# Windowed attention, forward and backward on one core: DMA-turned P and dS at both ends, reordered first loads and tail, W copies shared with VectorE

## The chip, the core and the metric

The kernel runs on one core of a Trainium2 chip. A core has a matrix engine (TensorE, PE in the profile, with its weight loads shown apart as PEld), a vector engine (VectorE, DVE), a scalar engine (ScalarE, ACT), GpSimd (POOL) and a sync engine (SyncE, SP) that only issues transfers. ACT and POOL also issue transfers, each from its own queue. Matrix products land in PSUM, from where DVE or ACT copies them to SBUF, the on-chip memory.

The metric is the time of one execution on the device in microseconds (us). The profile is one execution recorded by the hardware profiler.

## The reference

Input `x` is an image of 256 x 256 positions with 384 channels, in bf16. It is cut into 1024 windows of 8 x 8 positions, 64 tokens each, and every window attends to itself with one head of 384 channels. The outputs are the forward result and the gradients of x, wqkv and wo for a given `grad_out`:

```python
xw = windows(x)                       # (1024, 64, 384)
qkv = xw @ wqkv
q, k, v = qkv[..., :C], qkv[..., C:2 * C], qkv[..., 2 * C:]
p = softmax(einsum('bqc,bkc->bqk', q, k) * C ** -0.5)
out = unwindow(einsum('bqk,bkc->bqc', p, v) @ wo)
...
_out, _vjp = jax.vjp(_f, x, wqkv, wo)
_grads = _vjp(grad_out)
```

## The kernel before

**The algebra.** The four weight blocks are folded first. `A` is the scaled product of the q and k blocks and `B` that of the v block with wo; their transposes are `AT` and `BT`. With them scores are x A x^T, and the kernel never forms q, k and v. In the code, `z` and `y` are projections of grad_out and x (lines 155-167), `uq` and `vq` are x times B and x times AT (`uv`, lines 227-235), `sd` holds scores and dP together (`scores`, lines 180-187), `P` is the softmax, D its row sum with dP, and dS the gradient of the scores (`soft`, lines 192-225).

**The tiling.** Four pairs of windows make a quad: a tile of 128 partitions (two windows of 64 tokens) times QUAD = 4. There are 128 quads. In most tiles of a quad the lower 64 partitions (LO) belong to the first window of a pair and the upper 64 (HI) to the second.

**The pipeline.** Step i works on three quads at once: attention of quad c = i - 1, scores, softmax and uv of quad b = i, and projections of quad a = i + 1 (`step`, lines 346-387). The order in which each engine does things is written out by hand: the whole body stands under a manual schedule, and each engine runs its instructions in the order in which the program issues them. A step starts with `scores` of b on PE; then follow the eight uv products with softmax between them on DVE and ACT; the three z products of a; the last softmax stage and `turn` (lines 237-245); the loads of quad i + 3; the three y products; one row of weight-gradient products when there is one (`gf_rows`, 308-314, `pg` in the profile); and attention of c, four rounds t = 0 to 3 (`attend`, 254-298). `attend` computes three banks a round, `pw`, `pu` and `po`, and an edge bank `pd`. pw is copied to Wq by ACT (line 280), pu to Uq by DVE (line 283), po to the output by ACT (273), and pd by DVE and ACT in turn.

**PSUM.** All products take their banks from one ring of eight (line 58). When a bank isn't yet copied out, the next product that needs it waits.

**Turning tiles.** Attention needs P and dS of a quad in transposed form, `PS`. Before, DVE makes it from `ps` (P and dS side by side) in five transposes of 32 x 32 blocks (lines 240 and 244). The transposed x and grad_out (`xT`, `dT`) come from DMA transposes on SP (`load_turn`, 135-141); for the first quads from PE transposes instead, with copies by `copy_out` that alternate between DVE and ACT (`turn_on_pe`, 143-148). G_ON_PE = 4 says that dT of quads 0 to 3 is made on PE, X_ON_PE = 1 that xT of quad 0 is. Token-major z and y (`tok`) come from one larger DMA transpose on SP a quad (`to_tokens`, 175-178), of 24 blocks of 128 x 128; xT and dT have 12 blocks.

**SP's queue in step i** is: dT and xT of quad i + 2, tok of quad i, and two of the four x loads of quad i + 3. The other two x loads are on ACT after y's copies (`load_rest`). POOL issues the grad_out loads (dq) and the stores. Each of these waits in order on its queue.

**Weight gradients.** Three finished quads form a group (GQ = 3). Each group leaves six rows of products, put into `fill` (line 472) when its last quad's attention is done. Each later step takes one by `gf_rows` and one spread over the attention rounds in half tiles (`gf_halves`, `ph` in the profile); DVE adds them to GF_acc in f32. The first group is complete at the end of step 3, so steps 0 to 3 have no such products. What is left after the last step is done in the `while fill` loop, and the last two quads' share in `gf_final`; `weight_gradients` (399-434) then forms the two weight gradients and stores them.

**The start** (lines 437-452): the weight loads, nine products on zeros that keep PE busy (`warm_up`), the loads of quads 0 to 2, the BT product, the PE turns of quad 0, the A product, the clearing of GF_acc. The loop starts at i = -1, which does only the projections of quad 0. B and AT are computed by `weight_rest` in step 0, between scores and uv (line 355).

Of the kernel before, what the change touches and what calls it, by code (L numbers as in the profile page):

```python
# [14 lines left out]
P = 128  # L15
# [8 lines left out]
def kernel(  # L24
# [50 lines left out]
    def fetch_weights():  # L75
        nc.sync.dma_start(out=w_sb[:, :, columns(2)], in_=w_in[:, :, columns(2)])
        nc.scalar.dma_start(out=wo_sb[:], in_=wo.rearrange("(m p) n -> p m n", p=P))
        for k in (0, 1):
            nc.scalar.dma_start(out=w_sb[:, :, columns(k)], in_=w_in[:, :, columns(k)])

# [31 lines left out]
    def weight_rest():  # L112
        weight_product(B_sb, wT[2], wo_sb, None)
        weight_product(AT_sb, wT[1], wT[0], scale)

# [5 lines left out]
    OTHER = {0: HI, WT: LO}  # L121

    def load(st, on_act=0):
        st["xq"] = xq = grp.tile([P, QUAD, C], BF16, tag="xq", name="xq", bufs=2 * GQ + 4)
        st["dq"] = dq = qp.tile([P, QUAD, C], BF16, tag="dq", name="dq", bufs=6)
        for t in range(QUAD):
            if t < QUAD - on_act:
                nc.sync.dma_start(out=xq[:, t, :], in_=windows(x, st, 2 * t))
            nc.gpsimd.dma_start(out=dq[:, t, :], in_=windows(grad_out, st, 2 * t))  # L129

    def load_rest(st, on_act):
# [60 lines left out]
    def soft(st, step):  # L192
# [23 lines left out]
        elif step == 4:  # L216
            st["pr"] = pr = sm.tile([P, QUAD, WT], F32, tag="pr", name="pr")
            for w, h in ((0, LO), (1, HI)):
                nc.vector.tensor_tensor(out=pr[h, :, :], in0=sd[h, :, w, :], in1=st["Pb"][h, :, :], op=ALU.mult)  # L219
            st["D"] = D = sm.tile([P, QUAD], F32, tag="D", name="D")  # L220
            nc.vector.tensor_reduce(out=D[:], in_=pr[:], axis=AX.X, op=ALU.add)
        else:
            pd = sm.tile([P, QUAD, WT], F32, tag="pd")
            nc.vector.tensor_tensor(out=pd[:], in0=st["Pb"], in1=over_k(st["D"][:]), op=ALU.mult)
            nc.vector.tensor_tensor(out=st["dS"], in0=st["pr"][:], in1=pd[:], op=ALU.subtract)

# [10 lines left out]
    def turn(st):  # L237
        ps = st["ps"]
        st["PS"] = dst = qp.tile([P, 2, QUAD, WT], BF16, tag="PS", name="PS")
        nc.vector.transpose(out=dst[:].rearrange("p s t k -> p (s t k)"), in_=ps[:].rearrange("p s t k -> p (s t k)"))  # L240
        for first in range(0, P, WT):
            for q in (0, SQ):
                k = SQ - q
                nc.vector.transpose(out=dst[first + k:first + k + SQ, :, :, q:q + SQ].rearrange("p s t k -> p (s t) k"),  # L244
                                    in_=ps[first + q:first + q + SQ, :, :, k:k + SQ].rearrange("p s t k -> p (s t) k"))

    def operand(st, n, t, h):
        if n in ("PT", "ST"):
            return st["PS"][h, int(n == "ST"), t, :]
        if n in ("z", "y"):  # L250
# [3 lines left out]
    def attend(st, t):  # L254
# [24 lines left out]
        slot(pw, ("Pb", "dq"), ("Pb", "z"), start=True)  # L279
        copies[EV["W"][t]](out=st["Wq"][:, t, :], in_=pw[:])  # L280
        pu = bank("pu")
# [64 lines left out]
    def step(c, b, a, ahead):  # L346


        def on(st):
            return (lambda f, *r: f(st, *r)) if st is not None else (lambda f, *r: None)  # L350
        C_, B, A = on(c), on(b), on(a)
        B(scores)
        B(soft, 0)
        if b is not None and c is None:
            weight_rest()
        B(uv, 0, 0)
# [20 lines left out]
        if ahead is not None:  # L377
            load_rest(ahead, ON_ACT)
        if fill:
            gf_rows(*fill.pop(0))  # L380
        slots = attention(c) if c is not None else iter(())
# [6 lines left out]

    G_ON_PE, X_ON_PE = 4, 1
    ON_ACT = 2  # L390
    EV = {"z": "AAA", "y": "AAA", "u": "AAAA", "v": "AAAA", "o": "AAAA", "U": "DDDD", "W": "AAAA", "d": "DADAA"}
    quads = [(row, col) for col in range(0, W, WIN) for row in range(0, H, 2 * WIN * QUAD)]
    sts = [{"at": q, "i": i} for i, q in enumerate(quads)]
    n = len(sts)
    AHEAD = 3
# [3 lines left out]
    def weight_gradients(group):  # L399
# [32 lines left out]
        for k in range(CK):  # L432
            product_row(k, dw[:, k, :], GFT[1], woT_sb, None)
            (nc.scalar, nc.sync)[k % 2].dma_start(out=dw_out[:, k, columns(2)], in_=dw[:, k, :])

    with tc.manual_schedule(engines=MANUAL):
        fetch_weights()
        warm_up(9)
        load(sts[0])
        make_identity(nc, ident[:])  # L440
        load(sts[1])
        load(sts[2])
# [4 lines left out]
        turn_on_pe(sts[0], "dq", "dT")  # L447
        turn_on_pe(sts[0], "xq", "xT")
        turn_blocks(wT[0], w_sb, 0)
        turn_blocks(wT[1], w_sb, CK)  # L450
        weight_product(A_sb, wT[0], wT[1], scale)
        nc.vector.memset(GF_acc[:], 0.0)
        held = []
        last = None
        get = lambda i: sts[i] if 0 <= i < n else None
        for i in range(-1, n + 1):
            if 0 <= i < n - 2:
                load_turn(sts[i + 2])
            if 0 <= i < n:
                to_tokens(sts[i])  # L460
            step(get(i - 1), get(i), get(i + 1), get(i + AHEAD) if i >= 0 else None)
            if 0 < i + 2 < G_ON_PE:
                turn_on_pe(sts[i + 2], "dq", "dT")
            if i == 1:
# [42 lines left out]
```

## Time and profile before

| | us |
|---|---|
| runs shown | 1910.97, 1917.22, 1922.25 (median 1917.22) |
| profiled execution, whole time | 1913.78 |
| its span, first to last instruction | 1912.0 |
| first scores (quad 0) start | 18.30 |
| scores of quads 1, 2, 3, 4 start | 30.5, 46.55, 59.87, 74.69 |
| scores of quads 5 and 6 start | 89.25, 103.82 |
| scores of quad 127 start | 1868.49 |
| first product of step 128 | 1883.5 |
| last attention product | 1889.6 |

| DMA transposes by SP | median us from issue to landing |
|---|---|
| tok | 10.3 (6.2 to 15.6) |
| xT | 7.6 (4.1 to 11.4) |
| dT | 7.2 (4.5 to 10.9) |

How to read it: an engine's busy time is the time in which it executes; a mean near the span doesn't say what a single step waits for. Rows of the timeline give start and length in us, the engine, the line of the kernel, the operation with output<-input, and its shapes; in brackets stands how long the engine was idle before it and what released it. "PEclk" is the granted clock of the matrix engine as a share of full speed. SPq and ACTq are transfers being issued; the time in such a row is the issue, not the transfer. The span is shorter than the whole time of its execution by 1.8 us.

### The profile page before, as it was taken

The numbers are of one execution on the slowest core, as the hardware profiler recorded it, in microseconds if no ns is written. First come the engines' busy times: TensorE is split into PE (matmuls) and PEld (weight loads), VectorE is DVE, ScalarE is ACT, GpSimd is POOL, SyncE is SP. The second block draws the span as 40 slices with busy tenths as digits, with TensorE's granted clock in tenths as the row PEclk, the third lists the DMA queues.
The fourth block names the chain that finished last, engine by engine and source line by source line (L and its number), as shares of the span: only waits on it lengthen the run. The fifth ranks groups of instructions, "written<-read, shape, count | busy, mean of one in ns | idle before, by whom it ended". The sixth has DMA issues, their size and how long they took to land.

```text
span 1912.0 us, 57287 instructions
## 1 busy us (share of the span) xinstructions
PE 1897.3 (99%) x22359; PEld 1131.5 (59%) x22359; DVE 1676.1 (88%) x3625; ACT 1530.4 (80%) x3357; POOL 860.0 (45%) x1574
## 2 busy tenths in 40 slices
PE   8999999999999999999999999999999999999998
PEld 5556655655665565556556655655665565556555
DVE  6888888888888888888888888888888888888887
ACT  7878887888788888878887887888788788878884
POOL 3444544444444444444444444444444444445432
PEclk9999999999999999999999999999999999999999
DMA  8999999999999999999999999999999999999993
GB/s 183 200 223 215 221 211 214 232 210 222 200 232 211 225 204 229 217 223 216 224 210 212 225 226 219 206 220 221 223 214 216 223 224 204 210 231 222 206 197 93
DMA packets 943376, 406.91 MB, mean 213 GB/s; under 512 B 825344, under 2 KB 918528, under 8 KB 943104
## 3 DMA queue, kind: packets, MB, share of 16 engines
q1 hardware_dynamic: 830352, 226.46, 77.1%
q0 software_dynamic: 75264, 151.11, 32.6%
q10 hardware_dynamic: 37488, 25.67, 6.0%
q8 instruction: 175, 2.87, 0.7%
q14 instruction: 97, 0.79, 0.1%
HBM read 101.84 MB, written 101.84 MB: 107 GB/s over the span
## 4 chain that ended last, share of the span: by engine, by line
PE 95%; DVE 2%; DMA 1%; ACT 1%; issue 0%; ACTq 0%; SPq 0%
PE pj L151 50%; PE pg L151 13%; PE ph L324 13%; PE sd L151 5%; PE pw L269 5%; PE po L269 4%; PE pu L269 4%; DMA dT<-dq 1%; PE pd L269 1%; DMA xq<-in_x_dram 0%; DVE PS L244 0%; ACTq L133 0%; PE pe L403 0%; DVE pr L219 0%; DVE Uq L283 0%
## 5 line engine op out<-in xcount | busy, mean ns | idle before, releaser
L289 POOL DMA_DIRECT2D out_dram<-o x512 | 274.4, 536 | 795.4 <-ACT o L273 783.6
L280 ACT CAST Wq<-pw 128x384 bf16<-128x384 f32 x512 | 246.6, 482 | 280.7 <-PE pw L269 264.9
L151 PEld LDWEIGHTS <-xT 128*128 128x128 bf16 x3072 | 292.3, 98 | 182.9 <-issue 1.0
L129 POOL DMA_DIRECT2D dq<-in_grad_out_dram x512 | 270.6, 534 | 194.5 <-PE pj L151 86.8
L151 PE MATMUL pj<-B_sb,xT 128*128 128x384 bf16 x1536 | 334.0, 327 | 0.0
L151 PE MATMUL pj<-AT_sb,xT 128*128 128x384 bf16 x1536 | 333.8, 326 | 0.0
L283 DVE CAST Uq<-pu 128x384 bf16<-128x384 f32 x512 | 283.1, 553 | 16.9 <-PE pu L269 4.9
L291 POOL DMA_DIRECT2D out_dram<-d x480 | 277.8, 579 | 16.3 <-ACT uq L235 6.6
L151 PE MATMUL pj<-dT,BT_sb 128*128 128x512 bf16 x1152 | 269.5, 379 | 0.0
L151 PE MATMUL pj<-xT,A_sb 128*128 128x512 bf16 x1152 | 269.5, 379 | 0.0
L269 PE MATMUL pd<-tok,ps 64*64 64x384 bf16 x2048 | 256.4, 327 | 0.7 <-ACT Wq L280 0.6
L165 ACT CAST yz<-pj 128x512 bf16<-128x512 f32 x384 | 224.8, 586 | 37.2 <-PE pj L151 28.6
L273 ACT CAST o<-po 128x384 bf16<-128x384 f32 x512 | 249.3, 487 | 3.8 <-PE po L269 3.6
L235 ACT CAST vq<-pj 128x384 bf16<-128x384 f32 x512 | 247.1, 483 | 3.7 <-PE pj L151 0.5
L235 ACT CAST uq<-pj 128x384 bf16<-128x384 f32 x512 | 244.4, 477 | 3.6 <-PE pj L151 1.8
L167 ACT CAST yz<-pj 128x512 bf16<-128x512 f32 x384 | 225.1, 586 | 23.5
L244 DVE STREAM_TRANSPOSE PS<-ps 32x256 bf16<-32x256 bf16 x512 | 223.2, 436 | 9.7
L151 PEld LDWEIGHTS <-xq 128*128 128x128 bf16 x1572 | 153.6, 98 | 115.0 <-issue 0.6
L324 PEld LDWEIGHTS <-xq 64*64 64x64 bf16 x6000 | 177.5, 107 | 67.0
L324 PE MATMUL ph<-Wq,xq 64*64 64x384 bf16 x3984 | 204.4, 322 | 0.0
L151 PEld LDWEIGHTS <-A_sb 128*128 128x128 bf16 x1152 | 112.7, 98 | 135.9
L151 PEld LDWEIGHTS <-BT_sb 128*128 128x128 bf16 x1152 | 112.7, 98 | 122.3
(85 smaller groups left out, 3066.1 us busy)
## 6 DMA issues: line engine op xcount, KB each, us to landing
dq<-in_grad_out_dram POOLq DMA_DIRECT2D x512, 96.0 KB, 5.8
out_dram<-o POOLq DMA_DIRECT2D x512, 96.0 KB, 5.1
out_dram<-d POOLq DMA_DIRECT2D x480, 96.0 KB, 5.4
xq<-in_x_dram SPq DMA_DIRECT2D x262, 96.0 KB, 4.9
xq<-in_x_dram ACTq DMA_DIRECT2D x250, 96.0 KB, 6.0
out_dram<-d POOLq DMA_DIRECT2D x64, 48.0 KB, 5.4
tok<-zy SPq DMA_TRANSPOSE x128, 10.3
xT<-xq SPq DMA_TRANSPOSE x127, 7.6
```

The source lines that it names most:

```text
L129: nc.gpsimd.dma_start(out=dq[:, t, :], in_=windows(grad_out, st, 2 * t))
L151: nc.tensor.matmul(out, lhsT=lhsT, rhs=rhs, start=start, stop=stop)
L165: ENG[EV["z"][mo]](out=yz[:, mo, :, 0:4:3, :], in_=pj[:])
L167: ENG[EV["y"][mo]](out=yz[:, mo, :, 1:3, :], in_=pj[:])
L235: cp(out=dst[:, t, :], in_=pj[:])
L269: nc.tensor.matmul(dst[o, :], lhsT=operand(st, lhs, t, h), rhs=operand(st, rhs, t, h), **flags)
L273: copies[EV[name][i]](out=sb[rows, :], in_=src[rows, :])
L280: copies[EV["W"][t]](out=st["Wq"][:, t, :], in_=pw[:])
L283: copies[EV["U"][t]](out=st["Uq"][:, t, :], in_=pu[:])
L289: nc.gpsimd.dma_start(out=windows(out_0, st, 2 * t), in_=o)
L291: nc.gpsimd.dma_start(out=windows(out_1, st, 2 * t - 1), in_=d if t else above[:])
L324: nc.tensor.matmul(dst[o, :], lhsT=st["xq"][h, t, ma * P + o.start:ma * P + o.stop], rhs=st["UW"[f] + "q"][h, t, :], start=(i == 0), stop= ...
```

## The change

Seven things are done:

- P and dS of quads 0, 1, 2 and 127 (`crossed`) are turned by one DMA transpose on SP instead of by DVE. For this a tile `cr` is filled in the last softmax stage: two half copies of P by ACT and two half subtractions by DVE, with the halves exchanged; dS in `ps` is computed as before. `operand` reads the two halves of PS in exchanged order for these quads.
- dT of quads 2 and 3 comes from DMA transposes (G_ON_PE is 2).
- The weight loads are cut and shared between SP and ACT, the q and k blocks are loaded after quad 0's grad_out, quad 0's x after that; POOL waits with one-column copies for certain landings before it issues more loads. Within `load`, grad_out is issued ahead of x.
- The start projects quad 0 itself, z before the q and k blocks are turned, and the loop starts at 0. Warm-up has seven products; ACT makes a one-column copy early; GF_acc is cleared by POOL.
- `weight_rest` turns the finished BT and A on PE instead of computing B and AT as products, and stands before the scores of quad 0.
- For quads 0, 1 and 2 the W copies of rounds 0 and 2 are on DVE.
- In the last two steps two rows of `fill` are taken by `gf_rows` instead of one. The queues of the last three stores are exchanged.

```diff
     def fetch_weights():
-        nc.sync.dma_start(out=w_sb[:, :, columns(2)], in_=w_in[:, :, columns(2)])
-        nc.scalar.dma_start(out=wo_sb[:], in_=wo.rearrange("(m p) n -> p m n", p=P))
-        for k in (0, 1):
-            nc.scalar.dma_start(out=w_sb[:, :, columns(k)], in_=w_in[:, :, columns(k)])
+        wo_in = wo.rearrange("(m p) n -> p m n", p=P)
+        nc.sync.dma_start(out=w_sb[:, 0:2, columns(2)], in_=w_in[:, 0:2, columns(2)])
+        nc.scalar.dma_start(out=w_sb[:, 2, columns(2)], in_=w_in[:, 2, columns(2)])
+        nc.scalar.dma_start(out=wo_sb[:, 0:2, :], in_=wo_in[:, 0:2, :])
+        nc.sync.dma_start(out=wo_sb[:, 2, :], in_=wo_in[:, 2, :])
+
+    def fetch_rest():
+        nc.sync.dma_start(out=w_sb[:, :, columns(0)], in_=w_in[:, :, columns(0)])
+        nc.scalar.dma_start(out=w_sb[:, :, columns(1)], in_=w_in[:, :, columns(1)])
...
     def weight_rest():
-        weight_product(B_sb, wT[2], wo_sb, None)
-        weight_product(AT_sb, wT[1], wT[0], scale)
+        turn_blocks(B_sb, BT_sb)
+        turn_blocks(AT_sb, A_sb)
...
+    def load_first(st):
+        st["xq"] = xq = grp.tile([P, QUAD, C], BF16, tag="xq", name="xq", bufs=2 * GQ + 4)
+        st["dq"] = dq = qp.tile([P, QUAD, C], BF16, tag="dq", name="dq", bufs=6)
+        for t in range(QUAD):
+            (nc.sync, nc.scalar)[t % 2].dma_start(out=dq[:, t, :], in_=windows(grad_out, st, 2 * t))
+        fetch_rest()
+        for t in range(2):
+            nc.sync.dma_start(out=xq[:, t, :], in_=windows(x, st, 2 * t))
+        nc.gpsimd.tensor_copy(out=spare[:, 0:1], in_=dq[:, QUAD - 1, 0:1])
+        for t in range(2, QUAD):
+            nc.gpsimd.dma_start(out=xq[:, t, :], in_=windows(x, st, 2 * t))
+        nc.gpsimd.tensor_copy(out=spare[:, 1:2], in_=xq[:, 1, 0:1])
...
         else:
             pd = sm.tile([P, QUAD, WT], F32, tag="pd")
             nc.vector.tensor_tensor(out=pd[:], in0=st["Pb"], in1=over_k(st["D"][:]), op=ALU.mult)
+            if st["crossed"]:
+                st["cr"] = cr = qp.tile([P, QUAD, 2, WT], BF16, tag="cr", name="cr", bufs=1)
+                for w, h, o in ((0, LO, HI), (1, HI, LO)):
+                    nc.scalar.copy(out=cr[h, :, w, :], in_=st["Pb"][h, :, :])
+                    nc.vector.tensor_tensor(out=cr[o, :, w, :], in0=st["pr"][h, :, :], in1=pd[h, :, :], op=ALU.subtract)
             nc.vector.tensor_tensor(out=st["dS"], in0=st["pr"][:], in1=pd[:], op=ALU.subtract)
...
     def turn(st):
         ps = st["ps"]
         st["PS"] = dst = qp.tile([P, 2, QUAD, WT], BF16, tag="PS", name="PS")
+        if st["crossed"]:
+            whole = dst[:].rearrange("p s t k -> p (s t k)").rearrange("p (t s k) -> p t s k", t=QUAD, s=2)
+            st["PS"] = whole.rearrange("p t s k -> p s t k")
+            nc.sync.dma_start_transpose(out=whole.rearrange("p t s k -> p t (s k)"),
+                                        in_=st["cr"][:].rearrange("p t w k -> p (t w k)"))
+            return
         nc.vector.transpose(out=dst[:].rearrange("p s t k -> p (s t k)"), in_=ps[:].rearrange("p s t k -> p (s t k)"))
...
-            return st["PS"][h, int(n == "ST"), t, :]
+            return st["PS"][h, int((n == "ST") == (h == LO or not st["crossed"])), t, :]
...
-        copies[EV["W"][t]](out=st["Wq"][:, t, :], in_=pw[:])
+        copies[EV["W"][t] if st["i"] >= GQ else "DA"[t % 2]](out=st["Wq"][:, t, :], in_=pw[:])
...
+        if b is not None and c is None:
+            weight_rest()
         B(scores)
         B(soft, 0)
-        if b is not None and c is None:
-            weight_rest()
...
-        if fill:
-            gf_rows(*fill.pop(0))
+        for rows in range(1 if a is not None else 2):
+            if fill:
+                gf_rows(*fill.pop(0))
...
-    G_ON_PE, X_ON_PE = 4, 1
+    G_ON_PE, X_ON_PE = 2, 1
...
-    sts = [{"at": q, "i": i} for i, q in enumerate(quads)]
-    n = len(sts)
+    n = len(quads)
+    sts = [{"at": q, "i": i, "crossed": i < GQ or i == n - 1} for i, q in enumerate(quads)]
...
-            (nc.scalar, nc.sync)[k % 2].dma_start(out=dw_out[:, k, columns(2)], in_=dw[:, k, :])
+            (nc.sync, nc.scalar)[k % 2].dma_start(out=dw_out[:, k, columns(2)], in_=dw[:, k, :])
...
+        spare = sm.tile([P, 3], BF16, name="spare", bufs=1)
         fetch_weights()
-        warm_up(9)
-        load(sts[0])
+        warm_up(7)
+        nc.scalar.copy(out=spare[:, 2:3], in_=B_sb[:, 0, 0:1])
         make_identity(nc, ident[:])
+        nc.gpsimd.memset(GF_acc[:], 0.0)
+        load_first(sts[0])
         load(sts[1])
...
         turn_on_pe(sts[0], "dq", "dT")
-        turn_on_pe(sts[0], "xq", "xT")
+        for mo in range(CK):
+            project(sts[0], 0, mo)
         turn_blocks(wT[0], w_sb, 0)
         turn_blocks(wT[1], w_sb, CK)
         weight_product(A_sb, wT[0], wT[1], scale)
-        nc.vector.memset(GF_acc[:], 0.0)
+        turn_on_pe(sts[0], "xq", "xT")
+        gather(sts[0], 0)
+        for mo in range(CK):
+            project(sts[0], 1, mo)
+        gather(sts[0], 1)
+        turn_on_pe(sts[1], "dq", "dT")
...
-        for i in range(-1, n + 1):
+        for i in range(n + 1):
...
-            step(get(i - 1), get(i), get(i + 1), get(i + AHEAD) if i >= 0 else None)
-            if 0 < i + 2 < G_ON_PE:
-                turn_on_pe(sts[i + 2], "dq", "dT")
+            step(get(i - 1), get(i), get(i + 1), get(i + AHEAD))
```

More of the change, by code (lines that the diff above doesn't have):

```diff
@@ L126, in load @@
         for t in range(QUAD):
-            if t < QUAD - on_act:
-                nc.sync.dma_start(out=xq[:, t, :], in_=windows(x, st, 2 * t))
             nc.gpsimd.dma_start(out=dq[:, t, :], in_=windows(grad_out, st, 2 * t))
+        for t in range(QUAD - on_act):
+            nc.sync.dma_start(out=xq[:, t, :], in_=windows(x, st, 2 * t))
     def load_rest(st, on_act):
```

## The prediction

> **What bounds the kernel now.** I read first the page's busy shares, then the busy time cut at the start of each step's scores (L187), then the waits of PE, the timeline around the stalls and SP's own.
>
> ```profile
> PE 1897.3 (99%) x22359; PEld 1131.5 (59%) x22359; DVE 1676.1 (88%) x3625; ACT 1530.4 (80%) x3357; POOL 860.0 (45%) x1574
> ```
>
> PE is the bound nearly everywhere; 14.7 us of the 1912.0 us span are idle. The next table (stretch, length, then busy us and count of PE, PEld, DVE, ACT, POOL, granted clock, DMA share, GB/s) says where:
>
> ```profile
> 0.00:18.30 18.30, 15.35 (x108) 8.42 (x109) 7.16 (x15) 9.76 (x18) 11.28 (x26) 1.00 0.99 238
> 18.30:30.50 12.20, 12.20 (x99) 7.30 (x97) 8.86 (x21) 10.08 (x22) 0.00 (x0) 1.00 0.73 144
> 30.50:46.55 16.05, 14.01 (x139) 8.40 (x136) 14.34 (x33) 12.93 (x31) 4.15 (x8) 0.89 0.82 156
> 46.55:59.87 13.32, 11.61 (x119) 6.25 (x117) 11.44 (x27) 11.38 (x25) 4.73 (x9) 0.99 1.16 159
> 59.87:74.69 14.82, 13.11 (x117) 7.11 (x117) 11.38 (x27) 11.87 (x26) 6.59 (x13) 0.89 1.18 225
> 74.69:89.25 14.56, 14.56 (x176) 8.69 (x177) 12.21 (x28) 11.74 (x26) 7.00 (x14) 1.00 1.18 202
> 1868.49:1883.52 15.03, 13.12 (x165) 8.07 (x158) 12.44 (x28) 8.90 (x21) 4.78 (x10) 0.89 0.60 121
> ```
>
> From 74.69 on a step is 14.56 us of unbroken PE, and no edit touches it. Steps 1 to 3 (rows three to five) have no GF products yet: without pg (1.95) and ph (4 x 0.65) their PE work is 14.56 - 4.55 = 10.0 us, yet they last 16.05, 13.32 and 14.82. Step 127 has 9.3 us of work (0.81 + 3.9 + 1.95 + 2.6) and lasts 15.03. The waits and the clock say why:
>
> ```profile
> PE po L269 <- DVE Uq L283: 4.6, 5, 1.8
> PE pu L269 <- DVE GF_acc L306: 1.9, 1, 1.9
> ```
> ```profile
> 44.00:46.00 2.00, 2.00 (x24) 1.47 (x17) 1.53 (x5) 1.93 (x5) 2.00 (x5) 0.50 1.07 201
> 60.00:62.00 2.00, 2.00 (x27) 1.51 (x25) 1.05 (x3) 1.13 (x3) 2.00 (x5) 0.50 1.12 274
> 1880.00:1882.00 2.00, 2.00 (x29) 1.42 (x25) 0.62 (x2) 1.24 (x3) 1.59 (x3) 0.50 0.24 65
> ```
>
> PE waits for PSUM banks that DVE frees late, and after three of the stalls the clock is 0.50 for about 3.4 us (0.66, 0.50 and 0.98 in the stretches 42 to 48), some 1.7 us of PE lost each. DVE is late because it runs softmax and then these, before attention's copies:
>
> ```profile
> 39.09 1.78 DVE L244 STREAM_TRANSPOSE PS<-ps 32x256 bf16<-32x256 bf16 x4
> 1875.80 0.71 DVE L240 STREAM_TRANSPOSE PS<-ps 128x512 bf16<-128x512 bf16 x1
> ```
>
> One turn by L240 and four by L244, 2.53 us a quad from the start of the one to the end of the other. So only the start and the tail can change.
>
> **Prologue and step 0.** Before, the w_sb third that PE needs first (288 KB) landed at 4.95; dq tiles held PE until 9.71, then came xT turns, A, z, y, and scores at 18.30; weight_rest (18 matmuls of 384 columns, 19.13 to 22.05) kept uv until 21.89. After, nothing but 576 KB of weights precedes dq; I take w2 at 4.4 (between 3.3, its issue end 1.2 plus the 2.1 of the tail's stores, and 4.95). The last dq tile is issued on ACT behind the landing of a w2 part, so it is issued by 4.9 and lands at 7.0 to 9.4 (plus 2.1, or plus the 4.5 of wo); I take 7.2, since little else is in flight. w1's load behind it holds ACT until about 5.4; ACT's first wT copy stood at 5.60. The early table load (1.28) lies before that. Then: dT turn to 7.9, copy to 8.3; z 9 x 0.213 to 10.2; 18 turns to 11.3; A waits for two ACT copies behind z's three, 11.4 to 13.3; xT turn to 14.0, its ACT copies behind A's to 14.75; y to 16.65; quad 1's dT turn (0.7) to 17.35; the new weight_rest, 18 turns at the 1.17 of L98, to 18.5. Scores stand at 18.5, 0.2 later than before, but uv follows at 19.4 instead of 21.89. Exp sits on ACT behind four uv copies, so rs comes at 22.45 instead of 25.03. Until scores of quad 1: uv to 23.3, z and y to 27.2, then y's ACT copies, pushed back by two new cr copies (0.4 each, from ACT's 0.42 for ex 128x256), to 28.4. Scores at 28.45 instead of 30.51: **-2.05**.
>
> GF_acc's memset goes from DVE (1.98) to POOL: its bounds by ident's memset (0.244 for 128 columns, with or without the 0.10 of a one-column memset) are 2.6 and 4.4 us; POOL would anyhow wait for the dq landing near 7.2, so nothing; without that cover up to 4.4 on dq(1). The new order inside load changes nothing: dq and xq go by different queues. dq(1) is issued at 9 to 11 behind two xq loads and lands by 13 to 16.5 (median 5.8); PE needs it at 16.65, so at worst 0.5. Quad 2's and 3's dT, two 12-block SP transposes, replace 0.83 us of PE each; they land (7.2 median) around 25 and 38, before z needs them at 33 and 46.
>
> **Steps 1 to 3.** Here DVE sets the period. From mx to the end of PS took 8.7 us (47.45 to 56.15); Uq2, the bank that frees po3, followed after five 0.56 to 0.59 copies, 3.3, and po3, scores and the start of mx add 1.25: 13.25 undisturbed. Crossed: 8.7 less 2.53, plus two half subtractions of 0.45 (pr's row), is 7.05; W0 and W2 add 1.15 on DVE (two ACT copies go, but ACT isn't last); 7.05 + 4.5 + 1.25 = 12.8. Step 1 keeps the woT turn, 0.5; step 3's own quad isn't crossed but still copies two W, 14.45. New: 13.3 + 12.8 + 14.45 = 40.55 against 44.19: **-3.65**. The old sum contains about two clock dips. The new steps still leave PE 2.8 to 4.4 us idle each, so I put 1.2 us of dips back: start -2.05 - 3.65 + 1.2 = **-4.5**.
>
> The turned tile: one SP transpose of 4 blocks. Its price from SP's rows:
>
> ```profile
> 34.32 1.44 SPq L140 DMA_TRANSPOSE xT<-xq  x1
> 46.85 6.99 SPq L177 DMA_TRANSPOSE tok<-zy  x1
> ```
>
> Per block 0.12 (1.44/12) to 0.41 (slowest xT, 4.90/12): 0.5 to 1.6 of issue, taken 0.8, as it follows a tok. Landing: 4.1 (fastest xT) to 15.6 (slowest tok), taken 5, as it is a third of an xT. It waits on SP for cr; queued behind it are two xq loads and the next dT, xT and tok. By my times SP issues PS of quads 0, 1, 2 at 26.5, 41.5 and 55.8, and attention wants them at 37, 50.3 and 63.3: margins 5.5, 3.8 and 2.5 past the landing, and for the tok before it (started at 22, 37, 51, landing 7.4 to 10.3) 3 to 5. So nothing, while these hold; past them each us late is one us of path.
>
> **Tail.** Quad 127's chain loses 2.53 and gains 0.9 on DVE; more, steps 127 and 128 each do one gf_rows more (1.95), the work that stood after attention (4.07 at 1889.53). PE: 0.81 + 3.9 + 3.9 + 4.6 from 1868.5 reaches 1881.7, plus 0.5 for DVE's ten copies; then 3.9 + 4.0: 1890.1 instead of 1893.5 for the same work, -3.4. Quad 127's tile, issued at 1876.7, has until 1885.6; no other DMA is then on SP. Uq3 of 127 was covered by the removed 3.9; now the first final product waits 0.3. Swapping the last dw queues frees ACT's copy from a 0.37 us issue, but the last store still leaves at about 1908.9: 0.1. Tail **-3.2**.
>
> Sum: -7.7. The profiled execution took 1913.78 (span 1912.0), so 1906.1; it lies 3.4 below the median of the runs. Against the mean of all four executions, 1916.06, it is **1908**, which I forecast.
>
> [...] All nine warm-up matmuls run at 0.427 us apart (4.02 for nine), twice the later 0.213; the turns at 4.95 already run fast. Now seven end at 4.2. [...] PE waits for dq there, so I keep zero.
>
> **Rivals.**
> - *The bound only changes hands* (0.20): W on DVE plus repeated dips eat steps 1 to 3, and PE stays as idle as before. For it: clean old steps are 13.25, only 0.45 above my 12.8; all three dips follow stalls near 1.2 to 1.9 us. Against: step 0 and the tail don't need that saving. Without the -3.65, and with the tail at -2: 1916.1 - 2.05 - 2 + 1.2, that is 1913.
> - *The turned tile comes late* (0.12, slower). Place: SP, PS behind tok. With tok at its slowest 15.6, it lands at 37.8, 52.6, 66.6, PS some 3 to 3.5 later: 4, 6 and 7 us past need, 17, and stalls of that length bring a dip each, 3 more: 1908 + 20 = 1928. It decides for slower than before once the lateness adds up to 7.7. For it: tok takes 10.3 median in the filled steps, and the DMA share is 1.16 to 1.18 there. Against: early toks land in 7.4, and the DMA share falls to 0.10 at 28 to 32.
> - *More is won* (0.06): no dips, dq at 6.5, tail -4: 1903.
>
> **Numbers.** Forecast 0.62, its own range 1904 to 1912. A measurement of this kernel (1911 to 1922) tells about 0.5%, 9.6 us, from nothing. The forecast sits on that edge at 1907.6, so I split it: 0.36 faster, 0.26 same. Faster 0.36 + 0.06, same 0.26 + 0.20, slower 0.12. The range, 1900 to 1919, takes in the unknown bounds and the spread of runs, and leaves out the late tile.
>
> **What would show it.** Right: uv of quad 0 near 19.4, scores of quads 1 to 4 near 28.5, 41.8, 54.6, 69 (plus a dip), no pg between quad 127's attention and the final groups, and 14.56 us steps between. Wrong: PE waits named PS or tok, half clock until 8, dq(1) after 16.65, or steady steps above 14.6.

## The result, and the profile after

Nine executions of the changed kernel took 1903.38 to 1915.88 us, median 1908.05; nine of the kernel before, beside them, 1910.97 to 1922.25, median 1913.05. The two medians are 5.0 us apart and the means 5.8; the ratio estimated from the runs is 0.9963, with a 95% interval of 0.9948 to 0.9978, which is about 7 us. So 5 to 7 us are gained, and the interval keeps clear of 1. Of the prediction's classes that is "same", a difference of less than 0.5%, to which it gave 0.46. The forecast was 1908. Executions that took over 1.5% more than the fastest of the same kernel are left out of every ratio, and of the medians of e5 and e9 below.

The profiled execution of the changed kernel took 1904.35 us, span 1902.6, so it lies 3.7 below its median. Its busy us (share of the span) and instructions of each engine:

```profile
PE 1889.1 (99%) x22333; PEld 1125.4 (59%) x22333; DVE 1668.2 (88%) x3616; ACT 1527.2 (80%) x3354; POOL 859.7 (45%) x1575
```

PE lost 8.2 us of busy time and the span lost 9.4. The whole is seen in the busy time cut by step; columns as before: stretch, length, busy us and count of PE, PEld, DVE, ACT, POOL, granted clock, DMA share, GB/s. The rows are the prologue, steps 0 to 4, step 127, and the rest of attention of quad 127:

```profile
0.00:18.91 18.91, 15.44 (x124) 9.31 (x125) 5.93 (x17) 10.87 (x22) 11.48 (x25) 1.00 0.91 223
18.91:28.55 9.64, 9.06 (x71) 4.91 (x68) 7.34 (x20) 8.44 (x19) 1.18 (x3) 1.00 1.04 206
28.55:42.04 13.49, 12.31 (x122) 6.54 (x123) 11.03 (x25) 10.51 (x25) 1.87 (x4) 1.00 1.08 197
42.04:54.80 12.76, 11.83 (x117) 6.06 (x114) 10.60 (x26) 11.20 (x27) 5.86 (x12) 1.00 1.13 239
54.80:68.64 13.84, 11.73 (x119) 6.16 (x115) 12.01 (x27) 11.22 (x25) 7.11 (x14) 1.00 1.12 213
68.64:83.20 14.56, 14.56 (x178) 8.69 (x174) 12.67 (x29) 11.67 (x26) 7.02 (x14) 1.00 1.18 210
1863.41:1876.04 12.63, 12.63 (x172) 8.10 (x169) 10.87 (x25) 9.04 (x23) 4.29 (x9) 1.00 0.89 142
1876.04:1884.07 8.03, 8.03 (x124) 5.06 (x121) 5.20 (x11) 4.49 (x12) 4.22 (x9) 1.00 0.36 100
```

Two things are to be seen. Steps 1 to 3 sum to 40.09 us, where the prediction had 40.55 and the kernel before 44.19. And the clock column reads 1.00 in every row, where before it read 0.89 in three: this execution has no drop of the clock at all. Step 127 is 12.63 us of unbroken PE instead of 15.03 with 1.9 idle.

Against the trace of before, the 9.4 us come from these places. Scores of quad 1 begin in three pieces around two waits of 0.29, so the step is closed here with the first uv product after them.

| stretch | before | after | difference |
|---|---|---|---|
| start to the first uv product of quad 1 | 31.33 | 29.25 | -2.08 |
| from there to the scores of quad 4 (74.62, 68.64) | 43.29 | 39.39 | -3.90 |
| from there to the scores of quad 127 (1868.72, 1863.41) | 1794.10 | 1794.77 | +0.67 |
| from there to the end of the span | 43.28 | 39.19 | -4.09 |

(Where the window is drawn close, the scores of quads 4 and 127 of the kernel before begin at 74.62 and 1868.72; the 74.69 and 1868.49 used until here are 0.07 late and 0.23 early.) What PE still waits for, longest totals first (engine, line, tile, releaser: us in total, times, longest):

```profile
PE pd L298 <- ACT o L302: 1.7, 2, 1.0
PE po L298 <- DVE Wq L309: 1.7, 2, 1.3
PE pd L298 <- ACT Wq L309: 1.2, 2, 1.0
```

The waits for Uq and GF_acc (4.6 and 1.9) are gone. Neither PS nor tok is among the releasers in this trace; in that of e12 below, with the same start, both are. The waits that took their place are short. Those for ACT's copies of `o` are in steps 1 and 2 (0.96 and 0.76), where the prediction had called ACT "not last"; those for DVE are in step 3 (1.28 and 0.41).

### The profile page after: what moved, and what is told of

Same layout as the page of the kernel before. It is cut to its first block, busy times and chain, and to the rows that moved or that the text cites. A ratio compares the mean times of both kernels' runs of the same rounds, so it can differ in the third digit from the quotient of the medians.

```text
span 1902.6 us, 57253 instructions
## 1 busy us (share of the span) xinstructions
PE 1889.1 (99%) x22333; PEld 1125.4 (59%) x22333; DVE 1668.2 (88%) x3616; ACT 1527.2 (80%) x3354; POOL 859.7 (45%) x1575
## 4 chain that ended last, share of the span: by engine, by line
PE 96%; DMA 2%; ACT 1%; ACTq 0%; DVE 0%; issue 0%
PE pj L169 51%; PE pg L169 13%; PE ph L353 13%; PE sd L169 5%; PE pw L298 5%; PE po L298 4%; PE pu L298 4%; DMA dT<-dq 2%; PE pd L298 1%; ACTq L151 0%; PE pe L433 0%; ACT yz L185 0%; DMA dq<-in_grad_out_dram 0%; DMA w_sb<-in_wqkv_dram 0%; PE pt L103 0%
## 5 line engine op out<-in xcount | busy, mean ns | idle before, releaser
L273 DVE STREAM_TRANSPOSE PS<-ps 32x256 bf16<-32x256 bf16 x496 | 216.2, 436 | 9.5
```

## The experiments

All start from the changed kernel, and all compute everything. A trace is one execution, so a length read from it is that execution's alone. By the times no single part is shown to carry the gain: the ratios of e1 to e4, e7 and e11, each with one part undone, are 0.9961 to 0.9975, where the changed kernel has 0.9963. The new order of the first loads, the place of the clearing of GF_acc and the queues of the last stores were not undone by themselves. "Dense stretch" is from the first scores of quad 0 to those of quad 4, 49.73 us in the changed kernel; "equal steps" is from the scores of quad 5 to those of quad 127, 1780.2 us; "tail" from there to the end of the span, 39.19 us.

### First quads turned by DVE again (e1)

```diff
-    sts = [{"at": q, "i": i, "crossed": i < GQ or i == n - 1} for i, q in enumerate(quads)]
+    sts = [{"at": q, "i": i, "crossed": i == n - 1} for i, q in enumerate(quads)]
```

> Quads 0 to 2 turn P and dS on VectorE again; the last quad still by DMA. Marks are starts of scores: in the changed kernel quad 1 at 28.6 us, quad 2 at 42.0, quad 3 at 54.8, quad 4 at 68.6. Theory (VectorE sets the period of steps 1 and 2, and the turn is 1.65 us net of it): quad 2 at 43.5, quad 3 at 57.7, quad 4 at 71.5, total 2.9 us longer. Rival (ScalarE's copies end last in these steps, and VectorE's gain lies behind them): quad 4 at 69.5 or earlier, total under 1 us longer.

Median 1907.78 of five, ratio to before 0.9961 (0.9947 to 0.9976). Scores of quads 0 to 4 at 19.14, 27.63, 43.23, 57.44, 71.15: within 0.4 of the places that the theory named, and a dense stretch of 52.01, 2.3 longer. But 1.71 us of clock, which the theory had not counted, are lost in it, in this row of the busy time (columns as above):

```profile
40.00:45.00 5.00, 4.62 (x61) 3.24 (x57) 4.11 (x10) 3.23 (x8) 4.81 (x9) 0.66 1.06 213
```

A clock of 0.66 over 5 us is 1.7 us lost. The whole dense stretch settles little: the runs e4 and e12 below have the first quads turned by DMA, and drops of the clock there too, and theirs are 51.17 and 52.72. Steps 1 and 2 alone, from the last piece of the scores of quad 1 to the scores of quad 3, tell more. They took 28.97 in e1, that is 27.26 without its drop, and 25.69 to 26.20 in the changed kernel, e3, e7, e10 and e12, which have the same code in these steps and no drop in them. So the DMA turn is worth 1.1 to 1.6 us in the two steps where the theory had 2.9, or 2.8 to 3.3 if the drop is counted to it. In e1 PE idles 1.15 us for DVE's Wq in each of steps 1 to 3. In the whole time the turn can't be told from nothing.

### W copies on ACT again (e2)

```diff
-        copies[EV["W"][t] if st["i"] >= GQ else "DA"[t % 2]](out=st["Wq"][:, t, :], in_=pw[:])
+        copies[EV["W"][t]](out=st["Wq"][:, t, :], in_=pw[:])
```

> All W copies of quads 0 to 2 on ScalarE again. Theory of the prediction (VectorE ends last, two W copies cost it 1.15 us a step): quad 2 at 41.0, quad 3 at 52.8, quad 4 at 65.6, total 3 us shorter. Rival (ScalarE ends last in steps 1 and 2, since its x loads and cr copies push its o copies back; two more copies at 0.38 each add to it): quad 3 at 55.5 to 56.5, quad 4 between 68 and 70, total 0 to 1.5 us longer.

Median 1908.92 (1903.57 to 1915.95), ratio 0.9967 (0.9948 to 0.9986). Step 1 took 0.57 us more than in the changed kernel, step 2 0.09 more, step 3 0.29 less: 0.37 in all. The large gain that my theory gave to the removal of this edit isn't there, which speaks for the rival, that ACT ends steps 1 and 2. The timeline of the changed kernel shows it in step 1 (start, length, engine, line, operation; ACTq is a transfer issued from ACT):

```profile
37.24 0.56 ACTq L151 DMA_DIRECT2D xq<-in_x_dram  x1
...
37.84 1.51 ACTq L151 DMA_DIRECT2D xq<-in_x_dram  x1
39.40 0.48 ACT L302 CAST o<-po 128x384 bf16<-128x384 f32 x1 [1.22 <-PE po L298]
```

ACT is held by the second x load from 37.84 to 39.35; the copy that frees the next bank starts at 39.40, and the next product of PE at 39.93, after 0.96 us of idling. Ahead of the load stand two new cr copies of 0.40 each. That the load makes ACT last is shown by e5 and e9 below, which take the x loads out of ACT's way: in both, step 1 takes 13.06 us (from the last piece of the scores of quad 1) and step 2 12.46, and PE waits there for DVE alone. In e9's step 1:

```profile
41.06 0.32 PE L298 MATMUL po<-uq,PS 64*64 64x384 bf16 x1 [0.42 <-DVE Wq L309]
```

With the loads on ACT the two steps took 13.12 to 13.44 and 12.49 to 12.81 in the changed kernel, e3, e7, e10 and e12. So ACT's lead over DVE is at most 0.4 us. In step 3 DVE is last (PE idle 1.28 for Wq), and there the edit doesn't help.

### dT of quads 2 and 3 on PE again (e11)

```diff
-    G_ON_PE, X_ON_PE = 2, 1
+    G_ON_PE, X_ON_PE = 4, 1
...
+            if i + 2 < G_ON_PE:
+                turn_on_pe(sts[i + 2], "dq", "dT")
             if i == 1:
```

> dT of quads 2 and 3 is made on PE again, at the end of steps 0 and 1, with two copies each on VectorE and ScalarE. Theory (0.83 us of PE and 0.62 us of VectorE on the path of each of the two steps): scores of quad 2 at 42.9 to 43.5 and of quad 4 at 70.2 to 71 after a start at 18.9, total 1.5 to 2 us longer. Rival (PE stands idle in those steps, so nothing): quad 4 at 68.4 to 69.2; SP's queue, with two turns of 12 blocks less, a little earlier.

Median 1907.41 (1905.86 to 1918.71), ratio 0.9967 (0.9947 to 0.9988). Steps 0 and 1 took 0.64 us more in all, the dense stretch 0.78 more, and in that a drop of the clock begins at 68.16, 1.4 us before its end: between the theory and the rival. How far such a number carries is told by the other runs. The runs e3, e7, e9 and e10 and the changed kernel itself have the same code in steps 1 to 3 or all but the same, and their dense stretches are 49.63, 49.32, 49.04, 49.81 and 49.73. They differ by 0.8, and e4 and e12, with the same code and drops in it, took 51.17 and 52.72; so parts as small as e2's and this one are not settled by the dense stretch of one trace. In steps 0 and 1, 23.77 us here, the five took 22.74 to 23.13.

### Quad 3 turned by DMA too (e6)

```diff
-    sts = [{"at": q, "i": i, "crossed": i < GQ or i == n - 1} for i, q in enumerate(quads)]
+    sts = [{"at": q, "i": i, "crossed": i <= GQ or i == n - 1} for i, q in enumerate(quads)]
```

> Quad 3 is turned by DMA too. Theory (step 3 took 13.84 us because VectorE still turns quad 3 there and copies two W): step 3 at 12.7 to 13.0, scores of quad 4 at 67.6 to 67.9 after a start at 18.9, later steps 14.56, total 1 us shorter. Rival (SP's queue is full by then and the tile comes late): step 4 above 14.7, nothing won.

Step 3 fell to 12.48 us from 13.84, as the theory said. Step 4 then took 18.53 instead of 14.56, and the median is 1910.52 (1904.12 to 1912.93), ratio 0.9966 (0.9945 to 0.9987). Where it went, in ACT's timeline of step 4:

```profile
76.29 4.81 ACTq L151 DMA_DIRECT2D xq<-in_x_dram  x2
81.14 0.48 ACT L309 CAST Wq<-pw 128x384 bf16<-128x384 f32 x1 [4.28 <-DMA dT<-dq]
```

Two x loads held ACT for 4.8 us; all copies of attention stood behind them, and PE idled 2.06 us and lost 1.7 us of clock after it. So in this trace what was gained by less work on DVE was given back by a transfer's place in ACT's order. That the edit brings this is not shown: e12 has such a hold of 5.8 us in step 3 without it, and the ten executions of e6 lost 0.95 us of clock on average, less than those of the changed kernel (1.5). The rival's late tile isn't there: quad 3's PS landed at 72.65 and was wanted at 78.31.

### The tail: one row, DVE's turn, and both (e3, e4, e12)

```diff
-        for rows in range(1 if a is not None else 2):
+        for rows in range(1):
```

> The last two steps take one row of weight-gradient products each, as before; the last quad is still turned by DMA. The stretch from scores of quad 127 to the end is 39.2 us in the changed kernel, 43.5 in the kernel before. Theory (PE reaches attention of step 127 1.95 us earlier, while VectorE is still in softmax of quad 127, so it waits 1 to 2 us, perhaps with a clock dip of 1.7): 40.5 to 43. Rival (the DMA turn alone takes away the wait): 39.2 to 39.6.

```diff
-    sts = [{"at": q, "i": i, "crossed": i < GQ or i == n - 1} for i, q in enumerate(quads)]
+    sts = [{"at": q, "i": i, "crossed": i < GQ} for i, q in enumerate(quads)]
```

> Quad 127 turns P and dS on VectorE; the two rows a step stay. Theory (VectorE reaches attention's copies 1.65 us later, and PE waits for them about 1 to 1.6 us): the stretch from scores of quad 127 to the end is 40.2 to 41 us, 42.5 with a clock dip. Rival (the two rows alone cover it, as PE comes 1.95 us later): 39.2 to 39.6.

Both edits together are e12:

> Both tail parts undone: quad 127 on VectorE and one row a step. The stretch from scores of quad 127 to the end was 43.3 us before, 39.2 in the changed kernel, 40.0 with one row a step, 40.5 with the last quad on VectorE. Theory (either part alone takes most of one wait, and only without both is the wait long enough for the clock to drop): 42.8 to 43.5, with a half-clock stretch. Rival (the two parts add up, 0.8 + 1.3, and the rest is from elsewhere in the tail): 41.1 to 41.6 without a drop.

| | tail, us | median of ten, us | ratio to before |
|---|---|---|---|
| changed kernel | 39.19 | | |
| e3, one row a step | 40.01 | 1910.71 | 0.9972 (0.9958 to 0.9987) |
| e4, quad 127 turned by DVE | 40.46 | 1909.09 | 0.9975 (0.9959 to 0.9991) |
| e12, both | 43.13 | 1911.63 | 0.9982 (0.9967 to 0.9996) |

One edit undone costs 0.8 or 1.3 us, both undone 3.9: they are not additive. The same tail took 39.1 to 39.4 in the eight other kernels that have it unchanged (39.8 in e8), so the differences stand clear of its spread. In e4 the second row of products covers most of DVE's turn, and PE waits only 0.8 us for GF_acc. In e12 nothing covers it. PE's wait in e12:

```profile
PE pu L298 <- DVE GF_acc L335: 1.9, 1, 1.9
```

and the clock in the windows after that wait (columns as above):

```profile
1879.00:1881.00 2.00, 1.57 (x20) 0.98 (x23) 1.85 (x4) 0.59 (x2) 0.38 (x1) 0.65 0.04 8
1881.00:1883.00 2.00, 2.00 (x32) 1.43 (x28) 0.71 (x2) 1.07 (x3) 1.21 (x3) 0.50 0.47 125
```

This is the wait and the drop of the kernel before, at the same place. 1.9 us of stall and about 1.7 us of clock are 3.6 of the 3.9. In the traces of e3 and e4 the stall stays under 1 us and no drop comes. Of the tail's 4.1 us the clock makes some 1.7. The other executions agree: one less the clock, times the span, is 3.4 us on average in e12's ten, 1.5 in the nine of the changed kernel. In the whole time e12's ratio lies 0.0019 above the changed kernel's, 3.6 us, though the intervals still touch. (e12 ran on another chip than e3 and e4; each ratio is to runs of the kernel before beside it.)

### The start: weight_rest, and the warm-up (e7, e10)

```diff
-        turn_blocks(B_sb, BT_sb)
-        turn_blocks(AT_sb, A_sb)
+        weight_product(B_sb, wT[2], wo_sb, None)
+        weight_product(AT_sb, wT[1], wT[0], scale)
```

> B and AT are computed as 18 products again instead of 18 turns, at the new place ahead of the scores of quad 0. Theory (this is the larger part of step 0's gain): 18 x 0.163 = 2.9 instead of 1.2 to 1.4 us, so scores of quad 0 at 20.4 to 20.6, quad 1 at 30.1 to 30.3, quad 4 at 70.2, total 1.6 us longer. Rival (PE would anyhow wait there for copies of VectorE and ScalarE): quad 1 at 28.6 to 29.2.

Scores of quad 0 at 21.18 instead of 18.91, those of quad 4 at 70.50 instead of 68.64: the theory's 70.2 within 0.3. The turns are worth 1.9 us by quad 4 in these two traces. In the other traces with seven warm-up products the scores of quad 0 start at 18.81 to 19.63, so their worth at that point is 1.6 to 2.4. The median, 1907.75 (1903.52 to 1914.44), ratio 0.9962 (0.9946 to 0.9978), shows none of it.

```diff
-        warm_up(7)
+        warm_up(1)
```

> One warm-up matmul instead of seven. [...] Rival (PE waits for loads and copies there, or needs no warm-up): scores of quad 0 at 18.9 to 19.6.

One execution, 1909.0 us. With one product to warm up, the first turns and the BT product run slower (timeline of e10):

```profile
4.08 1.14 PE L103 MATMUL pt<-ident,w_sb 128*128 128x128 bf16 x9 [2.27 <-DMA w_sb<-in_wqkv_dram]
...
6.01 2.72 PE L110 MATMUL pc<-wT,wo_sb 128*128 128x384 bf16 x8 [0.48 <-ACT wT L95]
```

and in the changed kernel, with seven:

```profile
4.15 0.69 PE L103 MATMUL pt<-ident,w_sb 128*128 128x128 bf16 x9
...
5.88 1.46 PE L110 MATMUL pc<-wT,wo_sb 128*128 128x384 bf16 x8 [0.60 <-ACT wT L95]
```

Nine turns 1.14 against 0.69, eight products 2.72 against 1.46; scores of quad 0 come at 20.63, 1.7 us later than in the changed kernel's trace and later than the rival's 18.9 to 19.6. So one product is too few, by 1.7 us in this trace. With seven no cost can be seen. The trace of the changed kernel is one of four of the twelve with seven products in which the nine turns took 0.69 to 0.75. In the eight others they took 1.16 or 1.17, as long as here, and the eight products behind them 1.46 to 1.94, so full pace came up to about 2.7 us later there, an estimate from these rows: 0.48 us longer is some three products at twice the 0.163 us of the fast ones, to 6.8 instead of 4.15. Even so z started at 8.77 to 9.59 in all twelve (10.58 here), and the scores of quad 0 at 18.81 to 19.63 in all but e7, the earliest of them in one of the eight. Where between one and seven it begins to cost was not tried.

### The turned tile late on SP (e8)

Four further 4-block turns of the same tile, whose outputs nothing reads, stand ahead of PS on SP for quads 0 to 2:

```diff
+            if st["i"] < GQ:
+                for k in range(4):
+                    extra = qp.tile([P, QUAD, 2 * WT], BF16, tag=f"ex{k % 2}", name="extra", bufs=1)
+                    nc.sync.dma_start_transpose(out=extra[:], in_=st["cr"][:].rearrange("p t w k -> p (t w k)"))
             nc.sync.dma_start_transpose(out=whole.rearrange("p t s k -> p t (s k)"),
```

> For quads 0 to 2 SP issues four unused turns of the same size ahead of the real one; in the changed kernel a turn was issued in 1.2 us and landed in 2.4 to 5.2. The tile is then 5 to 6 us later. Theory (margins of the changed kernel: landed at 31.5, 43.4, 57.0, wanted at 37.3, 50.8, 63.6, so 5.8, 7.4 and 6.6 us): quad 0's attention waits under 0.5 us, but SP's queue falls 5 us behind each step, so attention of quads 1 and 2 waits 2 to 6 us; quad 4 at 72 to 77. Rival (SP catches up, as it waits elsewhere anyhow): quad 4 at 68.6 to 69.5.

One execution, 1941.46 us. Its SP timeline and PE's waits:

```profile
50.21 10.10 SPq L269 DMA_TRANSPOSE extra<-cr  x4
60.36 1.27 SPq L270 DMA_TRANSPOSE PS<-cr  x1
```
```profile
PE pu L302 <- DMA PS<-cr: 11.8, 3, 5.1
...
PE pd L302 <- DMA tok<-zy: 6.1, 2, 3.2
```

Scores of quad 3 started at 68.41 instead of 54.80, those of quad 5 at 108.99 instead of 83.20: twelve more turns cost 25.8 us there. The other 11 of the 37 us by which the execution is longer lie almost all in the equal steps, which differ by as much without the turns (below). The four turns take so long because the third writes the buffer of the first (`extra` has two) and waits until that has landed, 9.6 us in three waits, by SP's own waits:

```profile
SPq L269 <- DMA extra<-cr: 9.6, 3, 4.4
```

The issue itself took 1.2 to 2.4 us a turn. The prediction's slow rival has the price of a late tile right in kind, with drops of the clock behind it (0.991 over the whole run), but not the order: it had tok late and PS behind it, and here PS is late first and the next tok behind it. One turn is cheap in the changed kernel, where SP is free:

```profile
27.95 1.22 SPq L266 DMA_TRANSPOSE PS<-cr  x1
```

In the changed kernel SP issues PS in 1.2 us, at 27.95, 39.78, 53.43 and 1870.97, and attention wants the first three at 37.3, 50.8 and 63.6. The four land after 2.4 to 5.2 us (median 3.4), at 33.12, 42.91, 57.04 and 1873.38.

The margin does not always hold. In e12, whose start is that of the changed kernel, SP issued quad 2's tile at 57.90 in 2.84 us, it landed at 64.71, and PE waited for it, and 0.56 us for tok just before. ACT's two x loads then held its copies from 63.08 for 5.8 us, PE idled for a copy behind them, and the clock fell for 6.8 us. PE's rows of e12:

```profile
64.75 0.35 PE L298 MATMUL pu<-xq,PS 64*64 64x384 bf16 x1 [0.53 <-DMA PS<-cr]
...
69.47 0.47 PE L298 MATMUL pd<-tok,ps 64*64 64x384 bf16 x1 [3.32 <-ACT o L302]
```

Step 3 took 17.16 us there instead of 13.84. So the rival of the late tile is real in one of the traces, at 0.5 us. In e9 the same tile landed 0.1 us before it was wanted, and in e5 PE waited 1.1 us for it. Why SP was later there is open.

### ACT's x loads elsewhere (e5, e9)

e6 suggests taking the x loads out of ACT's way. Two places were tried: behind attention's copies, and on GpSimd.

```diff
         for mo in range(CK):
             A(project, 1, mo)
-        if ahead is not None:
-            load_rest(ahead, ON_ACT)
...
         for rest in slots:
             pass
+        if ahead is not None:
+            load_rest(ahead, ON_ACT)
```

> ScalarE's two x loads of every step are issued after attention's copies instead of ahead of them. In the trace with two waits of 3.3 us and less inside the long run of equal steps, ScalarE stood in front of such a load while PE waited for its W copy. Theory (these loads wait for an earlier load's completion and hold ScalarE's copies; that is what makes some executions longer): from scores of quad 4 to scores of quad 127 1793.0 to 1793.8 us with no PE wait on ScalarE, quads 2 and 3 each 0.3 to 0.8 us earlier than 42.0 and 54.8 after a start at 18.9, and the median at 1903 to 1905, spread under 5 us. Rival (x tiles come too late then): PE waits before projections, steps above 14.6, 1910 or more.

```diff
-            nc.scalar.dma_start(out=st["xq"][:, t, :], in_=windows(x, st, 2 * t))
+            nc.gpsimd.dma_start(out=st["xq"][:, t, :], in_=windows(x, st, 2 * t))
```

> The two x loads a step that ScalarE issued are issued by GpSimd at the same place of the program. In the traces so far the long run of equal steps differs by up to 10 us between kernels that have the same code there, with PE waits on ScalarE's W copy behind such a load. Theory (a load in ScalarE's queue that waits holds the copies, and that is the spread): no such waits, quad 5 to quad 127 in 1777 to 1778 us, median 1901 to 1904, spread under 4 us. Rival (GpSimd's own queue is late, behind stores, so x tiles, then SP's turns and tok come late, as when ScalarE issued them last): PE waits on tok, median above 1915.

e5: median 1922.58 of seven (all twelve: 1910.86 to 1983.92), ratio 1.0043 (1.0016 to 1.0069), longer than before. e9: 1917.25 of ten (all twelve: 1907.73 to 1960.6), ratio 1.0013 (0.9982 to 1.0044), no gain. In both the rival was right in that PE waits longest for late tiles, in attention. The profiled executions took 1946.63 and 1926.98. PE's first wait in e5, and in e9:

```profile
PE pd L298 <- DMA tok<-zy: 17.9, 9, 4.7
```
```profile
PE pd L298 <- DMA tok<-zy: 12.3, 8, 2.7
```

The x loads feed SP's next xT; when they come later, SP waits for them with tok behind it. In e5 SP's waits for x tiles sum to 395.6 us, against 185.3 in the changed kernel; in e9 they are 209.6, so there this is not shown to be the whole reason. No version that was run beats the changed kernel clear of the intervals.

## Why the prediction was right, and where it was not

**The time.** 1908 was forecast and 1908.05 measured. That it was met so closely is luck: the forecast starts from 1916.06, the mean of four executions, while the median beside the changed kernel was 1913.05, from which the same sum gives 1905.4. The sum, -7.7, is somewhat above the measured gain of 5 to 7; the two traces differ by 9.4. The parts as undone one by one in the traces, 1.1 to 1.6 (e1), 1.9 (e7), 3.9 (e12) and under 1 each (e2, e11), make up most of that if they add. Some 2.3 of what lies between the traces and the runs is clock. A single drop costs 1.70 to 1.71 us in the traces of before, e1 to e3, e8 and e9, by the clock of their rows. The profiled execution of before has three, that of the changed kernel none. That none came was chance: nine traces have the first three quads turned by DMA and quad 3 by DVE, with at most one small edit in their start (the changed kernel and e2, e3, e4, e7, e9, e10, e11, e12), and they have 0, 1, 0, 2, 1, 0, 1, 1 and 2 drops in the first 90 us (e12's is one of double length), about one on average. The mean granted clock of each execution says the same, as far as its three digits go: one less the clock, times the span, is 4.3 us on average in the 88 executions of before that were run beside the experiments, and 1.5 us in the nine of the changed kernel. So some 2.8 us of the difference may be clock, not the 5.1 of the two traces; how much of a drop lies in time that PE would have idled anyway isn't told by it.

Here is one of them. In step 3 PE idles 1.28 us for a DVE copy, in the changed kernel (65.77) and in e2 (66.87) alike, and only in e2 does the clock fall. Busy time of e2:

```profile
65.00:70.00 5.00, 3.42 (x53) 1.83 (x44) 4.72 (x10) 3.81 (x11) 2.60 (x5) 0.82 1.21 275
70.00:75.00 5.00, 5.00 (x41) 3.20 (x39) 2.51 (x7) 3.94 (x11) 3.84 (x8) 0.84 1.18 301
```

**Prologue and step 0, -2.05.** Right: -2.08. Scores of quad 0 stood at 18.91 (18.5 predicted), uv at 19.61 (19.4), rs at 22.59 (22.45). z came 0.6 later than predicted, at 8.88, since the last dq tile was seen by POOL at 7.98, where its landing was put at 7.2. POOL's memset took 2.01 us, below the lower of the two bounds (2.6); it is hidden, as predicted. e7 shows that the turned weights are needed for it: with products in their place the last piece of the scores of quad 1 starts at 30.86, where before it was 30.51. Seven warm-up products in place of nine were priced at zero, and no cost of them is seen. No run with seven shows the half clock until 8 that was named as a sign against it: the eight BT products took 1.46 to 1.94 us, against 2.72 with one product (e10). What the reordered loads gave by themselves was not tried.

**Steps 1 to 3, -3.65.** Right as a sum (-4.1 by the steps' lengths), wrong in one step: "two ACT copies go, but ACT isn't last". In the changed kernel's trace ACT is last in steps 1 and 2, through its x loads and the cr copies, and DVE only in step 3. The working reached the right length by the wrong engine, which is partly luck: it counted 12.8 us for DVE's chain in step 2, and the step took 12.76 with ACT's load and copies as the last release; with the loads elsewhere (e5, e9) DVE ended it at 12.46. DVE is thus close behind, and the price put on its chain was 0.3 too high. The W edit, which the working charged with 1.15 on DVE, gained 0.7 in steps 1 and 2 and cost 0.3 in step 3 (one trace of e2).

**Dips put back, +1.2.** Zero in this trace, about 1.5 on average in the nine: the term had the right size and belongs to the runs, not to one profile.

**The turned tile.** Issue 1.2 us, where 0.8 was taken; landing 3.4 median, where 5 was taken. The margins past the landing were 4.2, 7.9 and 6.5 us, where 5.5, 3.8 and 2.5 were predicted. It cost nothing in this trace and 0.5 us in e12's, and e8 shows what it costs when the margin is gone. The rival's own sum is short: 17 us late and three drops at the prediction's 1.7 are 22, not 20.

**Tail, -3.2.** It was -4.1. The working added 0.5 us for DVE's ten copies in step 127 and 0.3 for Uq3; neither wait came. The 9.3 us of work that the prediction's first part gives step 127 don't fit its own terms in the tail, which make 11.3 with one row; measured, step 127 is 12.63 with two rows, less 1.95 for one of them some 10.7. Step 127 has no idle time, and the final products follow attention at once (PE of the changed kernel):

```profile
1883.82 0.32 PE L298 MATMUL po<-uq,PS 64*64 64x384 bf16 x1
1884.07 4.34 PE L169 MATMUL pg<-Uq,xq 128*128 128x384 bf16 x24
```

**The equal steps.** Predicted unaffected, 14.56 each; they are. But the stretch that is equal in code is not equal in time: 1779.5 us before and 1780.2 after, and 1777.5 to 1787.9 in e1 to e4, e6, e7 and e10 to e12. Parts worth 0.4 to 2.3 us vanish in that. The longest stretch, e3's, has its stall in the timeline of SP and ACT:

```profile
1522.29 4.50 SPq L158 DMA_TRANSPOSE xT<-xq  x1
```
```profile
1528.38 1.90 ACTq L151 DMA_DIRECT2D xq<-in_x_dram  x2
1530.32 0.48 ACT L309 CAST Wq<-pw 128x384 bf16<-128x384 f32 x1 [5.47 <-issue]
```

ACT's x load isn't issued until 1528.38; the copy of Wq stands behind it, and PE idles 3.26 us for it, with a drop of the clock after it. SP's issue of xT takes 4.50 there, 1.4 to 3.5 in steps 0 to 3 of the changed kernel. That a stall starts at ACT's x load is shown here, in e6 and in e12; why the load is held so long is not settled, and so neither is how to take the spread away.

## What to carry to other kernels

Before a wait is priced, look for the next engine that would end the step, and count the transfers that it issues as time of its own: here an x load on ACT, not the copies around it, set two of three steps, by up to 0.4 us. Where two edits remove one stall, undo both together as well as each alone, since either can hide it. And compare the clock of the profiled executions before comparing their spans: here three drops, 5.1 us, lay in one of two traces that differ by 9.4, and they come and go from run to run.

## What the runs showed of the hardware

- A single drop of the granted clock lasted 3.4 us at 0.50 and cost 1.70 to 1.71 us, after stalls of 0.97 (e4, at 40.53) to 3.3 us; in e12 one lasted twice as long, after 0.56, 0.53 and 3.32, and in e5 one from 321 to 329 cost 3.42. The stall of 1.27 to 1.28 us in step 3 was followed by one in e2, e4, e7, e10 and e11, and by none in the changed kernel, e3 and e9. One of 2.61 us was followed by a drop in e9, at 171.3, and by none in e7, at 669.4. So in these traces the length of a stall does not tell by itself whether a drop follows.
- A small transpose by DMA, of four blocks, took 1.2 us to issue where SP was free (changed kernel), and up to 2.8 in e12 and 3.3 in e5; it landed 2.4 to 5.2 us after its issue in the changed kernel, 6.8 in e12. Four in a row took 7.87 to 10.10 in e8, of which 2.4 to 4.4 were the third's wait for its buffer.
- A transfer issued from ACT is time of ACT: usually 0.54 to 0.6 us (median 0.57 in the changed kernel), but 1.5 for one (changed kernel, 37.84) and 1.9 (e3), 4.8 (e6) and 5.8 us (e12) for two where they were held, and the copies behind them waited.
